# Recurrent cross-attention into a Serf feed-forward: batch 1's states loaded and turned apart, first products over six banks, a new written order

## The chip, the cores and the metric

One core of a Trainium2 chip. The core has a matrix engine (TensorE, "PE" in the profile), a vector engine (VectorE, "DVE"), a scalar engine (ScalarE, "ACT"), GpSimd ("POOL") and SyncE ("SP"). SP, POOL and, for two loads, ScalarE also issue DMA transfers. Engines run their own instruction lists in order and meet only at semaphores. The metric is the device time of one execution in microseconds (us), the median of several runs.

## The reference

Two stages. Attention reads x (8 batches, 8 heads, 512 tokens, 64 wide) against 32 states per head, both ways, and the two results are stacked to 544 rows per batch. A feed-forward layer with h·erf(softplus(h)) follows, 512 to 2048 to 512.

```python
def _attn_ref(x, state):
    scores = scale * np.matmul(x, state.transpose(0, 1, 3, 2))
    a = softmax(scores)                      # with 1e-9 in the sum
    xread = np.matmul(a, state)
    scores2 = scale * np.matmul(state, x.transpose(0, 1, 3, 2))
    a2 = softmax(scores2)
    sread = np.matmul(a2, x)
    return np.concatenate([xread, sread], axis=2)

def _moe_ref(x, w_in, w_out):
    h = x @ w_in
    sp = np.maximum(h, 0.0) + np.log1p(np.exp(-np.abs(h)))
    g = h * erf(sp)
    return g @ w_out
```

(The two softmax lines stand for the reference's maximum, exponential and sum.) Between the stages x becomes (4352, 512): per batch 512 token rows and 32 state rows.

## The kernel before

**Everything is a named step.** Functions register steps (a name and a closure). A hand-kept string, ORDER, lists their names, and the program issues them in that sequence. `in_order` then ties each instruction to the one ahead of it on its engine. So ORDER fixes the list of every engine and DMA queue; across engines only data dependences hold. An entry `~k*n` issues n filler products of the identity into bank k; they compute nothing that is used. `warm` is eight more at the start.

**How the work is laid out.** PSUM has eight banks of 128 x 512. Weights arrive as 64-bit words and are converted in pieces: `i0` to `i3`, `o0` to `o3` for the first half of the hidden width, with loads `l0`, `l1` (SP, `load_raw`, line 385), two ScalarE passes `a0`, `a1` (lines 370, 372) and two VectorE passes `v0`, `v1` (374, 376); two pieces share a buffer of raw words, so `o0l1` waits until `i0` is converted. Batches run one after the other: first all eight with one half of the hidden width (steps `A1` to `A7`; batch 0 in its own way), then the states' rows (`SA`, `SB`), then all eight with the other half (`B0` to `B7`).

**Batch 0**, `attention0` and `first_unit`. `lx0` to `lx3` and `lst0` load it. `x0` to `x3` turn x on TensorE; `s0` (line 448) puts the states on both halves of the partitions; `q0`, `q1` are the scores, copied by `q00c` and so on; `tm`, `max`, `less`, `exp`, `sum`, `inv`, `norm`, `ta`, `tac` are one softmax and its turning. `big`, `wt`, `wz`, `wn`, `tw0`, `tw1` (line 461) and ScalarE's copies `tw0c`, `tw1c` are the other softmax, and `rd0` (line 524) reads x with it; `rn0`, `rt0`, `rc0` keep the result. `n00` to `n12` (line 945) multiply states by w_in; `h0` to `h7` (line 956) are the first products of the feed-forward, each into one bank, from which ScalarE takes softplus (`h0s`, line 676) and a copy (`h0c`); `h0e` is the erf of h0 and h1, `h0g` their product on VectorE. `o00` to `o36` (line 977) are second products: first digit the row block, second the piece of the weights.

**Batches 1 to 7**, `attention(b)`. `a1xq0` to `a1xq7` load x once more by heads (line 349, two SP transfers of 64 KB each), `a1tx` turns them on VectorE, `a1s` (line 549) is the scores from the turned states `st[:, 1]` into banks 6 and 7, `a1c0`, `a1c1` (559) copy them. A chain on VectorE and ScalarE makes both softmaxes, up to `a1ta0`, `a1ta1`. `a1x0` to `a1x3` load x plain, into the place that batch 0's x had. `A1m` (line 638) multiplies states and w_in into banks 6, 7, 1 and 2, `A1m00` to `A1m11` copy it out on ScalarE, `A1f01` and on (line 687) are seven-product blocks of the hidden layer, `A1ap`, `A1bp` (810) of the output.

**The states of batches 1 to 7.** `hold`, a one-element copy on POOL, reads what `norm1` wrote. Behind it on POOL `lst1` to `lst8` (`load_st`, line 360) load the states, one transfer per head for all seven batches. `u1` and `u0` (line 1041) turn them on TensorE, seven transposes into banks 5 and 4, `u1c` and `u0c` copy them back over `st` on VectorE. POOL's other transfers (line 718) add results in DRAM; they begin after 100 us.

**Line numbers of helpers:** 246 copies, 238 to 240 sums, differences and products, 423 fillers, 418 and 419 `inverse`.

Of the kernel before, what the change touches and what calls it, by code (L numbers as in the profile page):

```python
# [31 lines left out]
a1ta1 a1ey1 o00 y11 A1M2 A1f0c y12 a1ty0 A1f06 a1ty1 h4e A1f02 y13 a1kz A1M3 A1f0u2 a1x3 A1f05 y14  # L32
o2a1 a2xq6 h4g A1f07 o2a0 a2xq5 o02 t32 A1M4 A1f0u3 o2v0 A1f0c11 A1f0c22 A1f04 h6e o3v0 a1z0 A1f11
o3a1 a1z3 o2v1 a1z1 A1f03 a1z2 A1f0c21 yl1 a2tx0 o04 A1f1c o3v1 A1f16 A1f0c12 A1f0s12 A1f12 T2
A1f0s22 A1f1u2 rd1 A1f0s21 t11 a1iy A1f0s11 t04 A1f17 h6g a2x3 rn10 rn11 A1f1c11 rt1 A1f15 A1f1u3
t34 rc1 T4 A1f14 o24 A1f1c22 A1e0 t61 a2tx2 A1f13 t21 t41 a2s A1f1c12 A1f1s22 t22 o06 A1g0 A1f1s11
a3xq1 a2c1 t1k A1f1c21 o14 a2c0 A1f1s12 a2tu0 o0c A1f1s21 o16 o0d t12 a2mx0 a2x2 a3xq7 A1e1 a2my0
o30 t3k yk0 a2sb0 a3xq5 o26 a3xq2 A1g1 a2ex0 a3xq0 A2m a3xq4 a2sm0 a2x0 o32 A2m00 t62 a3xq3 a2iz
A2m10 t42 a2nm0 A2m11 t2k o2c o34 a3xq6 a2ey0 A2M1 A2m01 a2ta0 a2x1 a2ey1 o36 A2M2 y21 A1q A2f01
o3c A2f05 A2f0c a2ty0 o1c y22 A1ap50 A1A1 A2f06 y23 A1ap10 a2ty1 A2f0u2 A2M3 A2f02 a2kz a2iy y24  # L40
A2f07 t24 T3 A1ap11 A2f0u3 A2f0c11 A1A3 A1ap51 A1ac A2f04 A2f0c22 A2M4 A2f11 A2f0c21 a2z3 t33 t4k
A2f03 t03 A2f1c a2z2 t51 a2z0 a3tx2 A1ap20 a2z1 yk1 A2f16 A2f0c12 o2d A2f0s12 o3d A1A2 A2f12
A2f1u2 o1d A2f0s22 yl2 A2f15 t13 yk2 A2f1c11 t23 A2f17 t6k a3tx0 rd2 A2f1u3 A1A4 A2f14 rn21 a3x2
rn20 t52 A1b2 rt2 A1ap21 rc2 A2f1c22 a3s A1ac11 A1a2 A2f13 a3c0 a4xq3 t43 t64 A2f1c21 A1ap60 A1a3
a3c1 a4xq2 A1ap61 A2f1c12 a3x0 A1bp10 t5k a3tu0 A1au2 a4xq0 A2f1s12 A1bp11 A2f0s21 t14 A1ap70 a3x1
a3mx0 A2f1s21 a3x3 A1ap71 A2f1s11 a4xq6 A1a4 A2f1s22 A3m A2f0s11 a4xq7 t44 A1au3 a3sb0 a4xq5
A1ap40 A1ac22 a3ex0 A1ap41 a3my0 A1ap30 A1ac21 t63 a3sm0 A1bc A1ap31 A3m01 A3m11 A1bp60 A1b3 a3ey1
A1bp61 a3iz A1ac12 A3m10 A1bp20 a3ey0 a3nm0 A1d2 A1bp50 A1bu2 a4xq4 A3m00 t53 A1bp51 a3ta0 A1bp21
A1bp70 t54 A2e0 y31 A1bp71 A3M1 A3f01 a3ty1 A3f05 a3ty0 A1bu3 A3f0c A3M2 A1bp40 a3kz A2e1 y32
A3f02 y33 A3M3 A3f06 A1bc22 A3f0c11 A1b4+ A1bp41 A1b4 A3f0u2 A3f11 A1bc21 y34 A1bc11 a3iy A2g0  # L50
A3f07 A1bp30 a3z1 A3f0u3 a3z3 a3z0 A1bp31 a3z2 A3f04 A3f0c22 A1d0 A3M4 a4xq1 A2ap10 A3f0c21 A1bc12
A1d3 A3f1c A3f03 A2g1 A1d1 A3f16 A3f12 A3f0s11 A3f0c12 A3f1u2 A1D0 rd3 A2q A3f0s21 A3f17 rn31 A1U2
rn30 rt3 A1D1 A2A1 A2ap50 A3f1u3 A3f0s12 A3f15 a4tx2 rc3 A2ap11 a4tx0 A3f14 A2ac A1U3 A2ap51 A2a2
A1D2 a4s A2A3 A2ap60 a4c1 a5xq1 a4c0 A3f1c22 A2ap61 a5xq0 A1D4 A2a3 A3f1c21 A3f13 A2au2 A1D3 a4x0
A3f1s12 a4tu0 A2ap20 A3f1c11 a5xq6 A2ap70 A3f1s22 A2A2 A2ap71 a4mx0 a5xq7 A2ap21 A2au3 A2A4 A2ap40
A2ac11 A3f1s11 A2ap41 a4sb0 A2bp10 A3f1c12 a4ex0 A2bp11 A2a4 A4m A2ac21 a4sm0 A2bc yl3 A2ac22
A2bp20 yk3 a4x2 a4iz A3f0s22 A2b2 A2bp21 a5xq4 A3f1s21 A2ap30 a4nm0 A4m01 A2bp60 A4m10 A4m11 A2b3
A2bp61 A4m00 A2ap31 a4ta0 A2bu2 a4x3 A2bp70 a4my0 A2bp71 A4f01 A2ac12 a4ey1 A4M1 A2d0 A2bp50 A2bu3
y41 a4ey0 a4x1 A4M2 A2bp51 A2d2 A4f0c A2bp40 y42 a5xq5 a4ty1 A2bp41 A4M4 A4f06 A3e0 a4ty0 A4f02
y44 a4kz A2b4 A2D0 yl4 A4f05 A4M3 A4f0c11 y43 A4f0u2 A2bc22 A4f11 A3e1 A2b4+ A3g0 A4f07 A2bp30  # L60
A4f0u3 A2bp31 A2bc11 a4z0 A4f04 A4f0c22 a4z2 a5xq2 A3g1 A4f03 A4f0c21 a4z1 A3ap10 A4f1c a4z3
A2bc21 a5xq3 A4f16 A4f0c12 A2d3 A4f12 a4iy A2bc12 A4f0s22 A3q A4f15 A2d1 A4f1u2 A4f17 A2U2 A3A1
rd4 A4f1u3 a5tx0 A4f14 rn40 rn41 A4f0s21 rt4 A3ap11 a5tx2 rc4 A3ap50 A3ac A4f1c22 A4f1c11 A3ap51
A3A3 A2D1 A4f1c21 a5s A3a2 A3ap20 a5c1 a6xq1 A2U3 A4f0s11 A3ap60 A3a3 A2D2 a5c0 A4f1s11 A3ap61
A2D3 A3A2 a6xq3 A4f13 a5tu0 A3ap21 a6xq2 A3au2 A2D4 A3ap70 A4f1c12 A3ac11 A3A4 A3ap71 a5x3 A3bp10
a5mx0 a6xq0 A3au3 A4f1s12 A3bp11 A3ac22 A4f1s22 A3ap40 A4f1s21 a5sb0 A3ap41 A4f0s12 A3a4 A5m a5my0
a5ex0 A3ap30 A3ac21 A3b2 A5m00 A3ap31 A3bc a5sm0 a5ey0 A3bp60 a5ey1 A3ac12 A3bp61 a5iz A5m11 A3d0
A3b3 A3bp50 A3bu2 a6xq4 A5m10 a5nm0 A3bp51 A3bp70 a6xq7 A3b4 A3bp71 a5x2 A4e0 a5ta0 A3bp20 a6xq6
A3bp21 A5M1 A3D0 A5f01 a5x0 A3bu3 y51 A5m01 A5M2 A3bp40 A5f0c a5ty0 A4e1 A3bp41 A3b4+ A5f02 y52
a5iy a5ty1 A5f06 A3bc11 A3bc22 a5kz A3bc21 A5f05 A5M3 a5x1 A5f0c11 y54 a6xq5 A5f0u2 A3bp30 y53  # L70
A4g0 A5f07 A3bp31 A5f0u3 A5f11 A5M4 A5f04 A5f0c22 a5z1 A4ap10 a5z3 A4g1 A5f0c21 a5z2 a5z0 A5f03
A5f1c yl5 yk5 A5f16 A3bc12 A5f12 A4q A5f1u2 A3d1 A3d2 A5f17 A5f1c11 A5f0c12 rd5 A4A1 A5f0s22 A5f15
a6tx0 rn51 rn50 A5f1u3 A4ap11 a6tx2 rt5 A3D1 A5f14 A4ac rc5 A5f1c22 A4ap20 A3d3 A3U2 a6x2 A4ap21
# [1077 lines left out]
```

## Time and profile before

| | |
|---|---|
| median of 3 runs | 689.32 us (688.62 to 690.2) |
| the profiled execution's own time | 691.2 us |
| its span, first to last instruction | 689.1 us |
| mean granted TensorE clock | 0.994 |
| DMA | 87.15 MB, mean 126 GB/s |
| instructions | 13808 |

A line of the busy table gives an engine's busy time, its share of the span and its instructions. The timeline gives start, duration, engine, line and operation, output and inputs, a count, and in brackets the idle time ahead of it with what ended it; durations include the pipeline's drain, so successive starts tell the pace. A stage row gives the stage, its length, busy time of TensorE, of its weight loads, of VectorE, ScalarE and POOL with instruction counts, then the granted TensorE clock (1.00 is full), the share of time in which the 16 DMA engines were busy, and GB/s. The time that a transfer takes to land is counted from its issue.

### The profile page before, as it was taken

How to read it: one execution, taken by the hardware profiler on the slowest of the kernel's cores; microseconds unless marked ns; L12 is line 12 of the kernel's file. 1: busy time of each engine (PE TensorE's matmuls, PEld its weight loads, DVE VectorE, ACT ScalarE, POOL GpSimd, SP SyncE). 2: the span in 40 equal slices, each digit the busy share in tenths (PEclk: the TensorE clock that was granted, in tenths of full speed). 3: DMA queues.
4: the chain of work that ended last, by engine and by line, in shares of the span. 5: the costliest groups of instructions: out<-in, count | busy, mean ns of one | idle time of the engine just before them, and what ended most of it. 6: DMA issues, size and time to landing. Idle time of an engine off the chain costs nothing.

```text
span 689.1 us, 13808 instructions
## 1 busy us (share of the span) xinstructions
PE 678.0 (98%) x5569; PEld 588.7 (85%) x5569; DVE 590.7 (86%) x771; ACT 489.5 (71%) x763; POOL 89.0 (13%) x84
## 2 busy tenths in 40 slices
...
GB/s 297 208 166 181 95 160 232 144 113 194 171 119 245 158 176 134 146 258 139 177 237 170 89 86 71 68 65 53 46 70 44 72 17 100 18 68 16 78 54 123
DMA packets 145567, 87.15 MB, mean 126 GB/s; under 512 B 92512, under 2 KB 137824, under 8 KB 145504
## 3 DMA queue, kind: packets, MB, share of 16 engines
...
q10 hardware_dynamic: 544, 0.52, 0.2%
q14 instruction: 19, 0.16, 0.1%
...
## 4 chain that ended last, share of the span: by engine, by line
PE 94%; DVE 2%; DMA 2%; ACT 1%; POOL 1%; issue 0%; DVEq 0%
PE b L810 47%; PE b L687 27%; PE b L740 5%; PE b L638 4%; PE b L1017 4%; PE b L977 3%; PE b L956 2%; DMA st<-in_state_dram 1%; PE b L524 1%; PE b L549 1%; POOL st L360 1%; DMA big<-in_x_dram 1%; PE b L1041 0%; PE b L461 0%; DVE ring L239 0%; DVE z L574 0%
## 5 line engine op out<-in xcount | busy, mean ns | idle before, releaser
L718 POOL DMA_DIRECT2D out_dram<-res x67 | 80.1, 1330 | 572.6 <-DVE res L238 179.7
L810 PE MATMUL b<-big,ring 128*128 128x128 f32 x1196 | 151.4, 275 | 0.0
L810 PEld LDWEIGHTS b<-big,ring 128*128 128x128 f32 x1196 | 144.9, 192 | 4.0 <-ACT res L246 1.0
L246 ACT COPY ring<-b 128x512 f32<-128x512 f32 (+1 forms) x144 | 82.7, 584 | 89.4 <-PE b L687 64.8
L687 PE MATMUL b<-y,m 128*128 128x256 f32 x480 | 121.3, 381 | 0.2 <-DVE y L246 0.2
L246 ACT COPY res<-b 128x512 f32<-128x512 f32 (+2 forms) x125 | 64.4, 524 | 53.9 <-PE b L810 37.3
L687 PEld LDWEIGHTS b<-y,m 128*128 128x128 f32 x480 | 86.5, 190 | 12.9 <-ACT ring L246 1.5
L687 PE MATMUL b<-sy,m 128*128 128x256 f32 x360 | 91.9, 380 | 0.0
L240 DVE TENSOR_TENSOR ring<-ring 128x2048 f32<-128x2048 f32 (+1 forms) x36 | 77.8, 2166 | 9.3 <-ACT ring L695 8.2
L676 ACT ACTIVATE ring<-ring 128x512 f32<-128x512 f32 x128 | 77.0, 632 | 1.0 <-DVE ring L238 0.5
L687 PEld LDWEIGHTS b<-sy,m 128*128 128x128 f32 x360 | 65.0, 190 | 9.0 <-issue 1.1
L810 PEld LDWEIGHTS b<-ta,ring 128*128 128x128 f32 x548 | 67.8, 192 | 5.5 <-issue 3.4
L810 PEld LDWEIGHTS b<-big,ta 128*128 128x128 f32 x572 | 68.9, 192 | 3.4 <-ACT res L246 1.7
L810 PE MATMUL b<-big,ta 128*128 128x128 f32 x572 | 71.8, 275 | 0.0
L810 PE MATMUL b<-ta,ring 128*128 128x128 f32 x548 | 71.8, 276 | 0.0
L239 DVE TENSOR_TENSOR ring<-ring 128x1024 f32<-128x1024 f32 (+3 forms) x66 | 68.8, 1046 | 0.1
L238 DVE TENSOR_TENSOR ring<-ring,b 128x512 f32<-128x512 f32 (+1 forms) x72 | 47.1, 658 | 25.3 <-PE b L687 8.7
L695 ACT ACTIVATE ring<-ring 128x2048 f32<-128x2048 f32 x30 | 57.4, 1913 | 0.2
L238 DVE TENSOR_TENSOR res<-res,b 128x512 f32<-128x512 f32 (+2 forms) x60 | 35.9, 599 | 24.2 <-PE b L810 14.3
L246 ACT COPY b<-b 128x512 f32<-128x512 f32 (+2 forms) x63 | 34.4, 548 | 16.6 <-PE b L810 12.3
L238 DVE TENSOR_TENSOR res<-res 128x512 f32<-128x512 f32 (+1 forms) x56 | 42.0, 751 | 0.8
L238 DVE TENSOR_TENSOR ring<-ring 128x1024 f32<-128x1024 f32 (+1 forms) x35 | 39.8, 1141 | 0.2
...
## 6 DMA issues: line engine op xcount, KB each, us to landing
...
big<-in_x_dram SPq DMA_DIRECT2D x112, 64.0 KB, 3.1
big<-in_moe_w_in_dram SPq DMA_DIRECT2D x12, 512.0 KB, 5.4
big<-in_moe_w_out_dram SPq DMA_DIRECT2D x12, 512.0 KB, 5.5
kept_y<-y SPq DMA_DIRECT2D x8, 512.0 KB, 4.1
y<-kept_y SPq DMA_DIRECT2D x8, 512.0 KB, 4.7
```

The costliest lines, as they stand in the source:

```text
L238: add = lambda o, a, b: tt(o, a, b, op=ALU.add)
L239: sub = lambda o, a, b: tt(o, a, b, op=ALU.subtract)
L240: mul = lambda o, a, b: tt(o, a, b, op=ALU.mult)
L246: do[name] = lambda: f(*args)
L638: pe.matmul(out=to[j][k][Ns * p:Ns * p + Ns, :], lhsT=by, rhs=w_in[r, 4 * j:4 * j + 4, i, :], start=True, stop=True)
L676: act.activation(out=o, in_=i, func=ACTF.Softplus)
L687: pe.matmul(out=to[:, i], lhsT=xs[n - 1][:, q:q + P], rhs=ys[n - 1], start=(start and i == 0), stop=(i == 1), skip_group_check=True)
L695: step(u + "e%d" % o, lambda s=s: act.activation(out=s, in_=s, func=ACTF.Erf))
L718: nc.gpsimd.dma_start(out=to, in_=of, accum_op=ALU.add)
L740: pe.matmul(out=to[:, E2 * h:E2 * h + E2], lhsT=a[:, k // 2, k % 2], rhs=rhs[n][:, k], start=(start and h == 0 and k == 0), stop=(k == 3), ...
L810: pe.matmul(out=out_[:, P * j:P * j + P], lhsT=lhs[:, i], rhs=rhs[:, i], start=(start and j == 0 and i == 0), stop=(i == 1), skip_group_ch ...
L1017: pe.matmul(out=to[:, P * i:P * i + P], lhsT=xs[n - 1][:, i, k], rhs=ys[n - 1][:, k], start=(start and i == 0 and k == 0), stop=(k == 1), ...
```

## The change

1. Batch 1's states get a load of their own on SP, `ls1` (64 KB), into the unused slot `st[:, 0]`. `ub` places them, in the form that `st[:, 1]` had, into bank 2 with four products against a rearranged identity; `ubc` copies them to `st[:, 1]` on VectorE.
2. `load_st` brings batches 2 to 7 only. `hold` now reads `sc` of batch 1, which `a1c0` writes, and stands behind `h5c`. `u0`, `u1` turn three batches each into banks 6 and 7, between `A1f02` and `A1f05`.
3. `h0` to `h7` use banks 0 to 5 in turn in place of 0 to 2.
4. The whole ORDER string is new, 2,511 entries after 2,516. It has the same steps but for `ls1`, `ub`, `ubc`, and 32 fillers after 33. The first lines of either are shown.

```diff
 ORDER = """
-warm lx0 lx1 lst0 lx2 lx3 i0l0 i1l1 i1l0 i0l1 x0 x1 x0c i2l0 s0 x1c x2 s0c i2l1 q0 x2c x3 q00c
-i3l1 q01c i0a0 big0 tm0 x3c i0v0 i0a1 q1 i3l0 max0 q10c i0v1 q11c less0 a1xq6 ~7*5 tm1 i1a1 big1
-n00 max1 exp0 i0+a0 less1 sum0 exp1 a1xq2 n00c0 sum1 i0+a1 i1a0 inv0 inv1 norm1 i2a0 norm0 hold
-~6*19 ta1 i1v0 lst1 i2a1 ta0 n00c1 lst6 i0+v0 i1v1 lst3 ta1c lst2 ta0c i0+v1 lst7 i3a0 o1l0 ~0*6
-n02 i2v0 lst4 n01 big n02c0 lst8 i2v1 i3a1 ~2*3 h0 lst5 n01c1 o0l1 n01c0 i3v0 wt0 o0l0 n02c1 n10
-wt1 a1xq3 i3v1 h1 n10c0 o1l1 n10c1 a1xq0 y01 wz n12 h0s wn1 h0c u1 n12c1 h1s u0 u1c n12c0 h1c wn0
-a1xq4 tw1 y02 u0c tw0 h0e a1xq1 h2 tw1c h0g a1xq5 tw0c o0a0 rd0 a1xq7 o1a0 o0v0 o3l0 h4 rn0 y04
-o1v0 yl0 a1tx1 rt0 o3l1 h3 h2s a1tx0 h2c a1tx2 o1a1 a1tx3 h5 o0a1 o1v1 rc0 h4c o0v1 a1s h4s h3c h7
-T1 h3s a2xq4 a1c0 a1c1 t01 o2l0 a1tu0 h5c a2xq3 h6 h5s a1my0 h7c t0k a1mx0 h7s a2xq1 a1tu1 o10 h6s
-a1my1 a2xq0 a1mx1 a2xq2 A1m a1sb0 h2e t31 a1x0 a1sb1 a2xq7 h2g o20 a1ex0 a1x2 t02 a1ex1 a1sm0 a1x1
-A1m10 o22 o2l1 a1sm1 A1m01 A1m11 a1iz y03 a1ey0 a1nm0 o12 a1nm1 A1m00 h6c a1ta0 o3a0 A1M1 A1f01
...
+warm lx0 lst0 lx1 lx2 lx3 i0l0 i0l1 i1l1 i1l0 x0 s0 x1 s0c x0c x2 x1c i2l0 q0 x2c x3 q01c i2l1
+q00c i0a0 big0 tm0 x3c i0v0 ls1 i0a1 max0 q1 i0v1 q11c q10c less0 i3l0 ~7*5 tm1 big1 exp0 n00
+i0+a0 max1 i3l1 i0+a1 sum0 i1a0 less1 inv0 a1xq6 big exp1 norm0 n00c0 sum1 i1a1 ~6*13 ta0 inv1
+n00c1 norm1 a1xq4 ta0c i1v0 wt0 ~7*4 ta1 i0+v0 i2a0 i1v1 ub ta1c i0+v1 ~6*4 n02 a1xq1 i2a1 i2v0
+n01 o0l1 y01 n02c0 i2v1 wt1 o0l0 ~5*4 h0 a1xq0 n01c0 i3a0 n01c1 n02c1 a1xq5 n10 i3a1 i3v0 o1l0 h1
+n10c1 n10c0 i3v1 wz ~7*2 n12 h1s wn1 a1xq7 h1c h5 wn0 n12c0 h0s y02 o1l1 ubc a1xq3 n12c1 tw0 a1tx0
+h0e tw1 a1tx2 a1xq2 h0c h3 y04 tw1c o3l0 h0g tw0c o0a0 rd0 a1tx3 o0a1 o0v0 h4 a1x1 rn0 a1x3 o1a0
+o0v1 o3l1 o2l0 rt0 o1a1 h2 o1v0 a1tx1 rc0 a1x2 t01 a1s o1v1 yl0 h4s h6 h2s T1 a1c0 h5c hold a1tu0
+h5s h7 lst8 t31 a1c1 a1mx0 o2l1 lst5 h3s a2xq5 a1tu1 h2c o20 h3c t02 a2xq2 a1my1 h7c h6s t04 t0k
+a1mx1 h7s o00 a1sb0 a1sb1 h2e t32 A1m t3k y03 a2xq0 t34 h2g lst1 a1x0 lst2 a1ex1 a1my0 a2xq4 o02
+a1ex0 lst3 a1sm1 a1ey0 a2xq1 a1sm0 a1ey1 o22 a1iz a1nm0 h4c A1m00 a1nm1 a2xq3 h6c o10 a1ta0 A1m11
+a1ta1 lst7 A1m10 y11 o3a0 lst6 a1ty0 A1f01 lst4 a1ty1 A1m01 o12 A1M1 A1f0c a1kz o2a0 y12 a2xq6
+A1M2 A1M3 o2a1 A1f06 a1iy y13 A1f02 o2v0 A1f0u2 y14 u0 o2v1 A1f07 h4e A1M4 u1 t61 A1f0u3 A1f05 h4g
+A1f0c11 a1z2 A1f04 o3a1 a1z3 A1f0c22 a1z0 A1f11 a1z1 o3v0 A1f0c21 yl1 t11 h6e o24 a2xq7 o3v1 A1f1c
+u0c A1f16 a2tx0 A1f03 A1f0s11 u1c A1f1u2 A1f12 T2 A1f0s12 A1f17 A1f0s22 A1f0c12 A1f1c11 rd1 A1f1u3
+T4 A1f1s11 A1f15 rn10 t12 a2x2 rn11 A1f0s21 t21 t1k rt1 h6g A1f14 a2x0 yk0 o04 A1f1c22 A1e0 a2tx2
+A1f13 t62 rc1 t22 a2s A1g0 A1f1s22 o06 a3xq0 a2c1 a2c0 A1f1c12 a2x1 A1f1c21 yk1 o14 a2tu0 o0c
+A1f1s12 a3xq4 A1f1s21 t41 a2mx0 o26 a3xq5 a2my0 A1e1 o16 a2sb0 a2x3 t4k A1g1 o30 a3xq2 a2ex0 A2m
+a2ey0 a3xq3 a2sm0 a2ey1 a3xq6 t14 o32 a2iz A2m10 a2iy t2k a2nm0 A2m11 o2c A2M1 o1c o34 o2d A2m00
...
 
     def load_st(h):
         i, e = h // 2, h % 2
-        nc.gpsimd.dma_start(out=st[Ns * i:Ns * i + Ns, 1:B, D * e:D * e + D],
-                            in_=state[1:B, h].rearrange("b n d -> n b d"))
+        nc.gpsimd.dma_start(out=st[Ns * i:Ns * i + Ns, 2:B, D * e:D * e + D],
+                            in_=state[2:B, h].rearrange("b n d -> n b d"))
+
+    def load_st1():
+        nc.sync.dma_start(out=st[:, 0].rearrange("p (g d) -> p g d", g=2),
+                          in_=state[1].rearrange("(g h) n d -> (h n) g d", g=2))
 
 
 
...
             step("norm%d" % g, lambda g=g: mul(a[g], a[g], over(Z1[:, g])))
             step("ta%d" % g, four, tp[g], lambda c, g=g: A0[:, g, c].rearrange("p q n -> p (q n)"))
             step("ta%dc" % g, act.copy, y[0][:, g], tp[g])
-        step("hold", lambda: nc.gpsimd.tensor_copy(out=sn[:, 0, 0:1], in_=A0[:, 1, 0, 0, 0:1]))
-        for h in range(H):
-            step("lst%d" % (h + 1), load_st, h)
 
         def rest():
             for e in range(2):
...
         for e in range(2):
             step(name("c%d" % e), lambda e=e: act.activation(
                 out=sc[:, e], in_=bank[6 + e], func=ACTF.Copy, scale=scale))
+        if b == 1:
+            step("hold", lambda: nc.gpsimd.tensor_copy(out=sn[:, 0, 0:1], in_=sc[:, 0, 0:1]))
         parts = [(str(e), slice(e, e + n)) for e in range(0, 2, n)]
         a = lambda e: both[:, e].rearrange("p e (k n) -> p (e k) n", n=Ns)
         M = lambda e: M1[:, e].rearrange("p e k -> p (e k)")
...
                 mixed_part(g, f, n, to)
             for i in range(4):
                 k = 4 * g + i
-                to = bank[k % 3]
+                to = bank[k % 6]
                 step("h%d" % k, first, g, i, to)
                 step("h%ds" % k, soft, s[:, k], to)
                 step("h%dc" % k, act.copy, hs[:, k], to)
...
     for j in range(4):
         piece("i", j)
     rest0 = attention0()
-    for k, bs in enumerate((range(1, 5), range(5, B))):
-        def turn_states(bs=bs, k=k):
-            for n, b in enumerate(bs):
-                pe.transpose(out=o_bank[2 + k][:, P * n:P * n + P], in_=st[:, b, :],
-                             identity=ident)
-        step("u%d" % k, turn_states)
-        step("u%dc" % k, dve.tensor_copy, st[:, bs[0]:bs[-1] + 1].rearrange("p b t -> p (b t)"),
-             o_bank[2 + k][:, 0:P * len(bs)])
+    step("ls1", load_st1)
+
+    def turn_st1():
+        by = ident.rearrange("p (a e n) -> p e a n", a=2, e=2)
+        for g in range(2):
+            for e in range(2):
+                pe.matmul(out=bank[2][D * e:D * e + D, D * g:D * g + D],
+                          lhsT=st[:, 0, D * g:D * g + D], rhs=by[:, e], start=True, stop=True)
+    step("ub", turn_st1)
+    step("ubc", dve.tensor_copy, st[:, 1], bank[2][:, 0:P])
     seconds0 = first_unit()
     for j in range(4):
         piece("o", j)
...
     attention(1)
     sums_y(1)
     mixed("A1", 1)
+    for h in range(H):
+        step("lst%d" % (h + 1), load_st, h)
+    for k, bs in enumerate((range(2, 5), range(5, B))):
+        def turn_states(bs=bs, k=k):
+            for n, b in enumerate(bs):
+                pe.transpose(out=bank[6 + k][:, P * n:P * n + P], in_=st[:, b, :],
+                             identity=ident)
+        step("u%d" % k, turn_states)
+        step("u%dc" % k, dve.tensor_copy, st[:, bs[0]:bs[-1] + 1].rearrange("p b t -> p (b t)"),
+             bank[6 + k][:, 0:P * len(bs)])
     hidden("A1", 1, 1)
     sums_a("A1", 1, twice=TWICE < 2)
     seconds0()
```

More of the change, by code (lines that the diff above doesn't have):

```diff
@@ L32 @@
[L32 to L73, printed above, removed]
@@ new lines @@
+a3ex0 a4xq7 A1b2 A1ap30 a3sm0 A1ap31 A2f0s22 A3m A1b3 A1ac21 a3iz A1bc t63 A2f1s21 a3nm0 A1bp60
+A3m00 A1ac12 A3m10 A1bp61 A3m11 a3ta0 A1bp20 A1d3 A2f0s21 A1d0 A1bp21 A1bu2 a3x1 t53 A3m01 A3f01
+a3iy a3x0 a3ty0 A2f1s12 A1bp70 A3M1 A3f0c a3ty1 A2f1s22 A1bp71 t64 A1bp50 a3kz A1bu3 y31 A3M2
+A1bp51 a4xq4 y33 A3f02 y32 A2e1 t54 A3f06 A3M3 A1D0 t44 A3f05 A1bc22 A3f0u2 A1b4 A1bp40 A2e0 y34
+A1b4+ A3f07 A2g1 A1bp30 A3f0u3 a3z2 A1bp31 A3f0c11 a3z1 A3f04 a3z3 A3f0c22 a3z0 A3f11 yk2 A3M4
+A3f0c21 A1d2 A1bc12 A1bp41 A3f1c A2g0 A3f03 A1bc11 A1bc21 A3f16 A1d1 A3f12 A3f1u2 A3f0c12 A2ap10
@@ new lines @@
+A5f05 y53 A5f0u2 A3b4+ A3bc21 A3bp30 A5M4 yl5 A4g0 A5f07 A5f11 a5z1 A5f0u3 a5z2 A3bp31 a5z3
+A5f0c22 a5x1 A5f04 A3D0 a5z0 A3bc12 yk5 A4ap10 A4g1 A5f0c21 A3d1 A5f1c A5f03 A5f16 A5f0c12 A5f12
+A5f1u2 A3U2 A5f15 A4q A5f17 A5f0s22 a6tx0 A4ap50 A5f1u3 A5f0s21 A4A1 rd5 a6tx2 A5f14 A3D1 rn51
+a6x1 rn50 rt5 A4ap11 A5f1c22 rc5 A4a2 a6s A4ac A4A2 A5f13 a6c0 a7xq4 a6c1 A4ap60 A4A3 A5f1c11
+A5f0s11 A4ap61 A3U3 A5f1c21 A4ap20 A4a3 A3D3 A4au2 A4ap21 A5f1s12 A3D2 a6tu0 a7xq1 A5f1s22 A4ap70
+A3D4 A4ac11 A4A4 A4ap71 A4bp10 a6mx0 A4au3 A5f1s11 A4bp11 A5f1c12 A4ap40 a6sb0 a6x3 A4ap41 a7xq0
@@ new lines @@
+A7f01 y71 A5d0 a7my0 a7x0 A5bp50 A5d2 A7f0c A5bp51 A6e0 y72 A7M2 A7f02 y73 A7f06 A7M4 yk7 A5bu3
+y74 A7f05 A7M3 A7f0u2 A5bc22 A5bp40 A5b4 A7f07 A6g1 a7ey1 A5D0 A5bp30 A5bc11 A7f0u3 A5bp31 A7f0c11
+A7f04 a7ey0 A5bc12 A7f0c22 A7f11 A6g0 A7f0c21 A5bp41 A7f1c A7f03 A5bc21 A7f16 A5d1 A6q A7f12
+A7f1u2 A6ap10 a7ty1 A7f0c12 A7f17 a7ty0 A7f15 A7f1u3 A6A1 a7kz i5+a1 A6ap50 A7f1c22 A7f14 A5U2
+A5D1 A6ap11 A6a2 A7f13 A6ac A5U3 A6ap51 A6A2 A6ap60 A7f1s22 A6A4 A7f0s12 A6ap61 A7f1c11 a7z3
+A6ap20 a7z1 A7f1c21 A6a3 a7z2 A6au2 a7z0 A5D4 A6ap21 yl7 A6A3 A6ap70 A5D2 A6ac11 A7f0s21 A6b2
```

218 lines of the change are left out of this document (117 added, 101 removed).

## The prediction

> **What bounds the kernel now.** I read the page first: busy times and the chain that ended last.
>
> ```profile
> span 689.1 us, 13808 instructions
> ...
> PE 678.0 (98%) x5569; PEld 588.7 (85%) x5569; DVE 590.7 (86%) x771; ACT 489.5 (71%) x763; POOL 89.0 (13%) x84
> ...
> PE 94%; DVE 2%; DMA 2%; ACT 1%; POOL 1%; issue 0%; DVEq 0%
> ```
>
> TensorE is the bound: it is busy 98% of the span and 94% of the chain. The number of its real instructions hardly changes, so the time can fall only by its idle time, by slow clock, or by filler products. The waits of TensorE, longest first, say where it is idle:
>
> ```profile
> PE b L1041 <- DMA st<-in_state_dram: 4.1, 1, 4.1
> ...
> PE b L687 <- DVE y L246: 0.2, 1, 0.2
> ```
>
> Columns: total, times, longest. One wait counts: line 1041 (steps u1, u0, the turning of the states of batches 1 to 7) stands 4.1 us for the state loads. Around it the timeline, the chain's pieces and the stage table show:
>
> ```profile
> 16.84 0.58 POOL L486 COPY sn<-ring 128x1 f32<-128x1 f32 x1 [15.53 <-DVE ring L240]
> 17.36 5.78 POOL L360 DMA_DIRECT2D st<-in_state_dram  x8
> 26.22 0.66 PE L945 MATMUL b<-w_in,st 64*32 64x256 f32 x16
> 30.98 1.73 PE L1041 MATMUL b<-ident,st 128*128 128x128 f32 x7 [4.09 <-DMA st<-in_state_dram]
> 32.49 1.91 PE L461 MATMUL b<-ident,ring 128*128 128x128 f32 x8
> ```
>
> ```profile
> 22.18 8.66 DMA st<-in_state_dram
> ```
>
> ```profile
> 27.00:31.00 4.00, 0.02 (x1) 0.06 (x1) 0.42 (x1) 3.77 (x6) 0.00 (x0) 0.81 0.89 186
> 31.00:37.00 6.00, 6.00 (x19) 4.21 (x19) 3.71 (x6) 3.14 (x4) 0.00 (x0) 0.56 0.65 102
> ```
>
> POOL begins the eight state loads at 17.36, behind the step hold. The last of them lands 8.66 us after the last issue. TensorE had finished line 945 (n12) at 26.22 + 0.66 = 26.88 and starts u1 at 30.98. Stage rows give TensorE, weight loads, VectorE, ScalarE, POOL, then the granted clock. In 31 to 37 us the clock is 0.56 on average: TensorE is "busy" for 6.00 us but does 6.00 x 0.56 = 3.36 us of work at full speed. So the stall costs 4.10 us idle + 2.64 us slow clock = **6.74 us**. After that:
>
> ```profile
> 45.00:100.00 55.00, 54.84 (x306) 30.66 (x305) 52.97 (x83) 49.00 (x73) 0.00 (x0) 1.00 0.64 147
> 100.00:200.00 100.00, 100.00 (x968) 87.90 (x974) 98.19 (x128) 74.94 (x124) 12.20 (x10) 1.00 0.76 169
> 200.00:300.00 100.00, 100.00 (x932) 88.62 (x913) 97.61 (x124) 74.93 (x122) 13.30 (x11) 1.00 0.77 172
> ```
>
> TensorE never waits again at full clock, but VectorE is 96 to 98% busy too (52.97 of 55, 98.19 and 97.61 of 100). It is nearly a second bound up to 300 us.
>
> [...]
>
> **The change part by part, against the profiled execution's own 691.2 us (span 689.1, 2.1 outside it).** The median of the three runs, 689.32, is 1.9 lower; a saving is taken off both alike.
>
> (a) *Batch 1's states apart.* ls1 is one more load of 64 KB on SP, ahead of i3's loads and all a1xq loads. The bounds are its twin lst0 and the slowest load of that time (columns: KB each, us to landing):
>
> ```profile
> ring<-in_state_dram SPq DMA_DIRECT2D x1, 64.0 KB, 3.8
> ring<-in_moe_w_in_dram SPq DMA_DIRECT2D x4, 512.0 KB, 9.4
> 1.25 0.45 SPq L341 DMA_DIRECT2D ring<-in_state_dram  x1
> 5.29 6.39 SPq L385 DMA_DIRECT2D ring<-in_moe_w_in_dram  x4
> 6.25 0.66 PE L448 MATMUL b<-ident,ring 128*64 128x128 f32 x8
> ```
>
> It holds SP for 0.45 us. It stands behind two of the four loads that took 6.39 us from 5.29, so it is issued by 5.29 + 3.2 = 8.5 and lands between 12.3 (8.5 + 3.8) and 17.9 (8.5 + 9.4). ub stands behind n00, 13 fillers, ta0, 4 fillers and ta1. The ta-steps need norm, whose end released hold at 16.84 before, and take 0.95: ub is due near 18. Its wait is nothing by either bound, though by the slower one without cover; a microsecond more is rival C. ub itself is four products like line 448's four (0.66 us) but half as wide: 0.3 to 0.66, taken 0.45. One transpose less in u0 and u1 gives 0.12 back, since line 461's eight take 1.91 at half clock, 0.95 at full. ubc is one more VectorE copy of 128 columns (about 0.3 us), between wn0 and n12c1, hidden unless VectorE is late there.
>
> (b) *Fillers.* 33 before (5, 19, 6, 3), 32 after (5, 13, 4, 4, 4, 2). Five take 1.38 us with the drain, so one is about 0.24 us:
>
> ```profile
> 10.47 1.38 PE L423 MATMUL b<-ident 128*128 128x128 f32 x10
> ```
>
> (a) and (b) on TensorE: +0.45 - 0.12 - 0.24 = **+0.1 us**. n12 would end near 27.0.
>
> (c) *u1 and u0 leave the early path.* After n12 TensorE now runs h5, tw0, tw1, h3, rd0, h4, rt0, h2, a1s. The first thing to come late is rd0, which needs ScalarE's copies tw1c and tw0c:
>
> ```profile
> 26.10 0.60 ACT L676 ACTIVATE ring<-b 128x512 f32<-128x512 f32 x1
> 28.45 1.28 ACT L971 ACT_TABLE_LOAD   x1
> 29.74 1.06 ACT L971 ACTIVATE ring<-ring 128x1024 f32<-128x1024 f32 x1
> 33.59 0.59 ACT L246 COPY ring<-b 128x512 f32<-128x512 f32 x1 [2.80 <-PE b L461]
> 34.20 2.91 PE L956 MATMUL b<-y,m 128*128 128x512 f32 x4
> 37.05 1.10 PE L524 MATMUL b<-big,ring 128*32 128x64 f32 x64
> 40.01 3.60 PE L956 MATMUL b<-y,m 128*128 128x512 f32 x8
> 43.53 1.09 PE L549 MATMUL b<-big,st 64*32 64x512 f32 x16
> ```
>
> ScalarE worked without a gap from h0s (26.10) to the end of h0e (29.74 + 1.06 = 30.80), then idled 2.80 us. The same steps stand ahead of tw1c in the new order (h0c now behind h0e), so the two copies end near 30.8 + 2 x 0.59 = 32.0. TensorE: two h-steps take 3.5 us (40.01 to 43.53), one 1.75; 27.0 + 1.75 (h5) + 0.95 (tw0, tw1) + 1.75 (h3) = 31.45. So rd0 waits 0.5 us (nothing to 1.2). Then 32.0 + 1.05 (rd0) + 1.75 (h4) + 0.1 + 1.75 (h2) gives a1s at 36.6, against 43.53. Of these 6.9 us, 0.8 are u1 and u0, which now come later: **6.1 us** gained here. a1s also needs the turned a1xq loads. SP issues ten of them in 10.76 us and they land 3.1 us later:
>
> ```profile
> 11.81 6.30 SPq L349 DMA_DIRECT2D big<-in_x_dram  x4
> 24.46 10.76 SPq L349 DMA_DIRECT2D big<-in_x_dram  x10
> big<-in_x_dram SPq DMA_DIRECT2D x112, 64.0 KB, 3.1
> ```
>
> In the new order six go out behind i3l1 (four before, at 1.6 us each), so until about 21; then o0l1 and ten more, among three weight loads of 0.45. That ends between 33 and 34, lands near 36.5, and a1tx1 (0.6) follows: a1s at 36.6 to 37.3. I take 36.7, **6.0 us**.
>
> (d) *From a1s to A1f01*, which waited for VectorE in the run of before (57.36). ScalarE fills this stretch:
>
> ```profile
> 35.00:56.30 21.30, 21.30 (x152) 8.87 (x151) 17.77 (x30) 19.69 (x32) 0.00 (x0) 0.97 0.74 170
> 48.09 1.88 PE L977 MATMUL b<-ta,ring 128*128 128x512 f32 x4
> 49.90 1.95 PE L638 MATMUL b<-w_in,st 64*32 64x512 f32 x32
> 57.36 1.10 PE L687 MATMUL b<-y,m 128*128 128x256 f32 x4 [0.16 <-DVE y L246]
> ```
>
> ScalarE needs 19.69 of the 21.30 us between tw0c and A1f01's inputs. From 32.0 that is 51.7 without any gap and 53.3 with the gaps of before. TensorE has a1s (1.0, from 43.53 to the next h-step), seven h- and o-steps of 1.75 (line 977's, 48.09 to 49.90, is one) and A1m (line 638, 1.9): 36.7 + 1.0 + 12.2 + 1.9 = 51.8. I take 52.3. Ahead of A1f01 the new order has one o-step more (1.72) and the u-steps (0.8) not yet: gain 57.36 - 52.3 + 0.9 = 5.96 (5.0 to 6.6).
>
> (e) *The other states on POOL*, hold now behind a1c0 (ScalarE's copy of the scores). POOL has nothing else until past 100 us (0.00 busy in 45 to 100), so nothing queues behind hold but the loads themselves. a1c0 ends near 38.9; from hold's start to the landing it took 30.98 - 16.84 = 14.1 us, so the states are there at 53.0. u0 comes after A1f01, o12, A1f06 and A1f02. An A1f-step is four products of line 687, which the chain's pieces give in sixteens:
>
> ```profile
> 60.17 3.45 PE b L687 x16
> ```
>
> So 3.45 / 4 = 0.86 each, and u0 is due at 52.3 + 0.86 + 1.72 + 1.72 = 56.6. Cover 3.6 us; if it is gone, rival B's price holds. u0 and u1 write banks 6 and 7, emptied by A1m00 and A1m01 shortly before.
>
> (f) *Six banks for h0 to h7*: on three banks the h-steps met one wait, of the weight load alone:
>
> ```profile
> PEld b L956 <- ACT ring L676: 0.8, 1, 0.8
> ```
>
> TensorE's own list does not have it; taken as nothing, a gain of 0.8 to a loss of 0.2 (the wait for y).
>
> (g) *The new order from 60 us to the end* changes the sequence, not the set, of steps. The row of before is "no wait"; bounds nothing to 2 us, taken 0.1.
>
> Sum: 6.0 - 0.1 = **5.9 us**; profiled execution 685.3, median 689.3 - 5.9 = **683.4**. Own range: gain 4.6 to 7.0, 682.3 to 684.7.
>
> **The rivals.**
>
> *A. VectorE caps the gain.* For it: 45 to 300 us leaves it about 6 us idle in all, and its regained time is bounded: idle 3.58 us in 27 to 31 and 2.29 in 31 to 37, together 5.9, exactly what TensorE gains. Wherever the new order puts VectorE work a little earlier than TensorE's need, TensorE waits. Against: TensorE had only one 0.2 us wait for it. If half the regained time is lost again: gain 3, **686.3**.
>
> *B. The stall moves to u0, and the kernel is slower.* Place: u0, behind the landing of the eight POOL loads. [...] The decisive point is a landing later than 56.6, and for a loss one later than 56.6 + 3.3 = 59.9: 3.3 us idle plus 2.6 us slow clock eat the gain. That is 21 us after hold, against 14.1. At 5 us idle: 689.3 - 5.9 + 5 + 2.6 = **691.0**. Against: the transfers of that time load the DMA engines to 0.74 (the share in the row for 35 to 56.3), those of before stood beside 1.04:
>
> ```profile
> 17.00:27.00 10.00, 9.49 (x99) 4.97 (x97) 8.94 (x18) 9.40 (x16) 6.13 (x9) 1.00 1.04 260
> ```
>
> [...]
>
> *C. The split does not free ub.* ls1 is queued behind six loads of 512 KB; if it lands after 18 us, ub waits and everything behind it: 1.5 us, gain 4.4, **684.9**. Against: it is as small as its twin, and only the slower bound comes near.
>
> **How the numbers follow.** Forecast 0.60, A 0.17, B 0.13 (of it 0.04 near no change, 0.09 slower), C 0.06, and 0.04 that the reordered rest has waits that cost over 5 us (0.01 same, 0.03 slower). About 0.2% (1.4 us) is what this kernel's runs can tell from no change. Faster = 0.60 + 0.17 + 0.06 = 0.83, cut to 0.82 for the tail of A; same 0.06 (B and the rest give 0.05, A's tail the other 0.01); slower 0.12. The range leaves out the slower part of B and the last case and reaches from 681.8 (gain 7.5: no wait at rd0, h-steps better) to 688.3 (A at its worst).
>
> **What would show it.** u1's wait gone from TensorE's list; granted clock 1.00 in 27 to 45; a1s near 36.7, A1f01 near 52.3, u0 near 56.6 without a wait; last state landing near 53; TensorE's tail unchanged. Wrong if TensorE's list shows a new wait over 1 us, at u0 (B), at line 549 or 687 for VectorE (A), or at ub (C), or if a second stretch of clock 0.50 appears.

## The result and the profile after

| | median | runs |
|---|---|---|
| before | 689.53 us | 12 |
| changed kernel | 686.75 us | 12 |
| ratio | 0.996, 95% interval 0.9946 to 0.9974 | |
| again, in another session: before 689.32, changed | 686.13 us | 26 and 9 |
| its ratio | 0.9957, interval 0.9944 to 0.9971 | |

The change makes the kernel about 3 us faster (2.8 and 3.2), where 5.9 was forecast. One of its first twelve executions, the profiled one, took 3722 us for a reason that stays open; what follows reads another profiled execution of the same kernel, of 686.48 us.

The page of that execution, in the places that were shown of before (span, busy times, the chain by engine):

```profile
span 684.4 us, 13822 instructions
...
PE 676.4 (99%) x5574; PEld 587.9 (86%) x5574; DVE 592.0 (86%) x772; ACT 493.5 (72%) x766; POOL 87.8 (13%) x84
...
PE 93%; ACT 3%; DVE 3%; issue 1%; DVEq 0%; ACTq 0%
```

The 4.1 us wait for the states is gone. ScalarE and VectorE now hold 3% of the chain each. The waits of TensorE (total, times, longest):

```profile
PE b L427 <- PEq L1150: 0.8, 1, 0.8
PE b L980 <- DVE ring L240: 0.5, 1, 0.5
PE b L465 <- DVE ring L246: 0.4, 1, 0.4
PE b L690 <- ACT ring L246: 0.3, 1, 0.3
PE b L465 <- DVE ring L240: 0.3, 1, 0.3
PE b L525 <- ACT ring L246: 0.3, 1, 0.3
PE b L690 <- DVE m L239: 0.3, 1, 0.3
PE b L460 <- DVE big L246: 0.2, 1, 0.2
```

Before had one wait of 4.1 us and three of 0.2 to 0.5 us (the 0.8 us of the start, PEq, stands in both); now there are seven of 0.2 to 0.5 us. (Lines moved by one to four: 980 was 977, 690 was 687, 465 was 461, 525 was 524.) The timeline of TensorE and of POOL at the points that the prediction named:

```profile
12.67 0.45 PE L948 MATMUL b<-w_in,st 64*32 64x128 f32 x16
18.44 0.45 PE L1047 MATMUL b<-ident,st 128*64 128x64 f32 x8
27.26 1.98 PE L959 MATMUL b<-y,m 128*128 128x512 f32 x4
32.11 1.10 PE L525 MATMUL b<-big,ring 128*32 128x64 f32 x64 [0.27 <-ACT ring L246]
36.88 1.31 PE L550 MATMUL b<-big,st 64*32 64x512 f32 x16
47.58 5.42 PE L980 MATMUL b<-ta,ring 128*128 128x512 f32 x12 [0.45 <-DVE ring L240]
52.84 1.03 PE L690 MATMUL b<-y,m 128*128 128x256 f32 x4
55.84 1.10 PE L690 MATMUL b<-sy,m 128*128 128x256 f32 x4 [0.26 <-DVE m L239]
57.64 0.49 PE L1064 MATMUL b<-ident,st 128*128 128x128 f32 x3
60.52 1.13 PE L690 MATMUL b<-sy,m 128*128 128x256 f32 x4 [0.32 <-ACT ring L246]
```

```profile
39.55 0.18 POOL L563 COPY sn<-big 128x1 f32<-128x1 f32 x1 [38.24 <-ACT big L560]
39.67 4.71 POOL L360 DMA_DIRECT2D st<-in_state_dram  x8
```

From above: n00, ub, h5, rd0, a1s, o02 to o10, A1f01, A1f06, u0, A1f04. ub and u0 start without a wait. The stage table (stage, length, TensorE, weight loads, VectorE, ScalarE, POOL, clock, DMA share, GB/s):

```profile
27.00:31.00 4.00, 4.00 (x31) 2.26 (x16) 2.74 (x7) 3.97 (x7) 0.00 (x0) 1.00 0.79 187
31.00:37.00 6.00, 5.73 (x79) 2.57 (x83) 5.50 (x9) 5.98 (x9) 0.00 (x0) 1.00 1.00 261
26.00:52.00 26.00, 25.28 (x185) 11.18 (x184) 23.27 (x44) 25.64 (x42) 4.83 (x9) 1.00 0.95 235
45.00:62.00 17.00, 15.96 (x82) 9.06 (x82) 16.11 (x31) 16.57 (x26) 0.00 (x0) 1.00 0.82 174
```

The clock stays at 1.00 where it was 0.56. In 26 to 52 us ScalarE is busy 25.64 of 26 us: its list has almost no gap left. In 45 to 62 TensorE is idle 17 - 15.96 = 1.04 us, all of it in the three marked waits; before it stood 0.16 there. The chain of work that ended last says who set the pace. It leaves TensorE behind an h-step, runs on ScalarE from 26.33 to 48.22 us, then on VectorE up to A1f06, and comes back to TensorE there. Three of its pieces (start, length, engine, output and line):

```profile
26.33 0.60 ACT ring L679
48.24 1.29 DVE z L577 x2
55.84 1.12 PE b L690 x4
```

### The profile page after: what moved, and what is told of

It is laid out like the page before. It is cut to its first block, busy times and chain, and to the rows that moved or that the text cites. A ratio compares the mean times of both kernels' runs of the same rounds, so it can differ in the third digit from the quotient of the medians.

```text
span 3720.2 us, 13822 instructions
## 1 busy us (share of the span) xinstructions
PE 3714.4 (100%) x5574; PEld 2927.6 (79%) x5574; DVE 601.4 (16%) x772; ACT 502.8 (14%) x766; POOL 87.8 (2%) x84
## 4 chain that ended last, share of the span: by engine, by line
PE 100%; DVE 0%; DVEq 0%; issue 0%
PE b L813 46%; PE b L690 28%; PE b L743 5%; PE b L980 5%; PE b L641 4%; PE b L1020 4%; PE b L959 2%; PE b L427 1%; PE b L525 1%; PE b L550 1%; PE b L465 0%; PE b L948 0%; PE b L445 0%; PE b L535 0%; PE b L460 0%; PE b L1064 0%
## 5 line engine op out<-in xcount | busy, mean ns | idle before, releaser
L813 PEld LDWEIGHTS b<-big,ring 128*128 128x128 f32 x1196 | 742.4, 846 | 59.0 <-issue 57.5
L813 PE MATMUL b<-big,ring 128*128 128x128 f32 x1196 | 746.1, 951 | 0.0
L690 PE MATMUL b<-y,m 128*128 128x256 f32 x480 | 638.4, 1622 | 0.0
L690 PEld LDWEIGHTS b<-y,m 128*128 128x128 f32 x480 | 400.5, 869 | 156.3 <-issue 156.3
L690 PE MATMUL b<-sy,m 128*128 128x256 f32 x360 | 476.1, 1618 | 0.0
L813 PEld LDWEIGHTS b<-ta,ring 128*128 128x128 f32 x548 | 368.5, 907 | 28.3 <-issue 27.4
L690 PEld LDWEIGHTS b<-sy,m 128*128 128x128 f32 x360 | 295.9, 854 | 117.1 <-issue 116.7
L813 PE MATMUL b<-ta,ring 128*128 128x128 f32 x548 | 371.2, 1011 | 0.0
L813 PEld LDWEIGHTS b<-big,ta 128*128 128x128 f32 x572 | 324.6, 781 | 24.3 <-issue 24.3
L813 PE MATMUL b<-big,ta 128*128 128x128 f32 x572 | 325.5, 880 | 0.0
L980 PEld LDWEIGHTS b<-ta,ring 128*128 128x128 f32 x64 | 55.0, 879 | 109.4 <-issue 107.5
L743 PEld LDWEIGHTS b<-big,ring 128*128 128x128 f32 x104 | 72.6, 704 | 43.7 <-issue 43.7
```

Of the source, the lines that this page charges most:

```text
L690: pe.matmul(out=to[:, i], lhsT=xs[n - 1][:, q:q + P], rhs=ys[n - 1], start=(start and i == 0), stop=(i == 1), skip_group_check=True)
L743: pe.matmul(out=to[:, E2 * h:E2 * h + E2], lhsT=a[:, k // 2, k % 2], rhs=rhs[n][:, k], start=(start and h == 0 and k == 0), stop=(k == 3), ...
L813: pe.matmul(out=out_[:, P * j:P * j + P], lhsT=lhs[:, i], rhs=rhs[:, i], start=(start and j == 0 and i == 0), stop=(i == 1), skip_group_ch ...
L980: pe.matmul(out=bank[3 + r % 3], lhsT=s[:, k, P * r:P * r + P], rhs=wo[0].w[:, k, :], start=(k == 0), stop=(k == NT - 1))
```

## The experiments

**1. How much does before lose at u1?** Before, unchanged, was profiled five times more, beside the kernels below; e_banks has its order too.

> The kernel of before again, to see how much the stall at u1 varies. Theory 1: a wait of 2 to 4 us at u1 and, when it is under about 2.5 us, no stretch of half clock, so a loss between 2 and 6.7 us. Theories 2 and 3: the same 4 us and half clock as in the first profile, since they put the missing gain into the new kernel.

> Before, unchanged, another profile. Theory 1 (the stall at u1 is different in every execution, and its price sets the time): the wait at u1 lies between 1.5 and 4.5 us; span less (wait + slow-clock loss) is 682 to 683 us, as in the profiles so far (689.1 - 6.7; 687.1 - 4.7). Theory 2 (the stall is the same and something later varies): the wait is 4 us whatever the span.

> Before, unchanged, one more profile. The same as for the last: Theory 1: span less (wait at u1 + slow-clock loss) 682 to 683 us. Theory 2: a wait of 4 us whatever the span.

> Before, unchanged, another profile. Theory 1 (early loads land differently in each execution, and what they cost sets the time): waits of TensorE for states or for weights between 17 and 37 us, with slow clock, of 3 to 7 us in all, and span less these 682 to 683.5 us. Theory 2 (the first profile is typical): u1 waits 4 us and the span is 689 us.

> Before, unchanged, one more profile. As for the last: Theory 1: 3 to 7 us of waits and slow clock between 17 and 37 us, span less these 682 to 683.5 us. Theory 2: u1 waits 4 us and the span is 689 us.

The waits of b_again, and then those of b_p2:

```profile
PE b L1041 <- DMA st<-in_state_dram: 1.6, 1, 1.6
PE b L956 <- ACT m L246: 1.3, 1, 1.3
...
PE b L461 <- DVE ring L501: 0.3, 1, 0.3
```

```profile
PE b L956 <- ACT m L246: 1.6, 1, 1.6
PE b L524 <- ACT ring L246: 1.0, 1, 1.0
```

b_p2 has no wait at u1 at all. It waits at h0 for n02c0, because ScalarE stood for a load of w_in ahead of it (i3), and then loses to slow clock. ScalarE's timeline and the stage row show it:

```profile
22.45 1.12 ACT L370 ACTIVATE w_in<-ring 128x1024 f32<-128x1024 f32 x1 [1.57 <-DMA ring<-in_moe_w_in_dram]
```

```profile
24.00:27.50 3.50, 3.50 (x5) 0.96 (x6) 1.85 (x3) 2.44 (x6) 0.00 (x0) 0.51 1.00 316
```

All seven profiles of before's order, with the waits of TensorE between 17 and 37 us and what the clock took ((1 - clock) x length of its stage rows):

| | span | u1 | h0 | rd0, tw | slow clock | span less these |
|---|---|---|---|---|---|---|
| first profile | 689.1 | 4.1 | - | - | 2.6 | 682.4 |
| e_banks | 687.1 | 3.0 | - | - | 1.7 | 682.4 |
| b_again | 685.4 | 1.6 | 1.3 | 0.3 | - | 682.2 |
| b_p2 | 688.3 | - | 1.6 | 1.3 | 1.7 | 683.7 |
| b_p3 | 687.3 | 2.2 | 0.9 | - | 1.7 | 682.5 |
| b_p4 | 685.8 | 1.8 | 0.8 | 0.3 | - | 682.9 |
| b_p5 | 685.3 | 0.6 | 1.2 | 0.7 | - | 682.8 |

The right column lies within 1.5 us (0.7 without b_p2) while the spans lie 3.8 us apart; the span follows what is lost early. (Five of the seven also wait 0.3 us at line 945, which is left in the column.) So Theory 2 falls, and b_again's Theory 3 with it: the first profile was the dearest of seven, not a typical one.

Theory 1 holds in kind, but only in the wider form that b_p4 and b_p5 state, with every early wait counted. In its first form, the stall at u1 alone, it missed: b_again waits 1.6 us there where 2 to 4 were asked, b_p2 not at all, and the span less u1's wait and slow clock is 686.6 us in b_p2 and 683.4 in b_p3, where 682 to 683 were asked. b_p4 and b_p5 keep the stated 682 to 683.5, but lose 2.9 and 2.5 us where at least 3 were asked; b_p2's remainder, 683.7, lies just outside even so.

A median run of before has a span of about 689.4 - 2.1 = 687.3, so it loses 687.3 - 682.7 (mean of the right column) = **4.6 us**, not 6.74; the seven profiles lose 4.2 on average. What makes the loads land so differently was not tried.

**2. The changed kernel again.**

> The changed kernel again, for a profile with TensorE at its usual pace. Theory 1 (the mechanism holds, the price is smaller): 686 to 687 us, no wait of TensorE over 1 us, granted clock 0.998 or more, a1s between 36.5 and 39 us; what is missing of the 5.9 us lies in waits of 0.3 to 1 us at rd0, a1s and A1f01, and in a run of before that had lost more than usual. Theory 2 (VectorE or ScalarE caps the gain): TensorE waits 2 us or more in all for VectorE or ScalarE between 27 and 300 us. Theory 3 (the stall moved): one wait of 2 us or more at u0 or ub for a load.

686.13 us, and the profile above: no wait over 0.5 us, a1s at 36.88. Theory 3 falls, as ub and u0 do not wait. Theory 2 asks for 2 us or more of waits for VectorE or ScalarE after 27 us; there are 0.27 + 0.45 + 0.26 + 0.32 = 1.30 us, so its cause is there and its price is not reached. Theory 1 has the time, the clock and a1s right, and of its places rd0; the other waits stand at o02, A1f06 and A1f04, not at a1s and A1f01.

Counted like the seven, and with the late waits, this profile leaves 684.4 - 0.55 (0.28 at ta1, 0.27 at rd0) - 1.03 (the three waits after 45 us) = 682.8 us, within 0.1 of before's mean remainder. So what the changed kernel still waits accounts for what it did not gain, in this one profile.

**3. Its parts alone.** e_banks is before with one edit. e_split is before's order with the split; only the moved steps are shown:

```diff
-                to = bank[k % 3]
+                to = bank[k % 6]
```

```diff
- ... i2l1 i3l1 ... norm0 hold ~6*19 ta1 i1v0 lst1 ... ta0 n00c1 ... ~2*3 h0
+ ... i2l1 ls1 i3l1 ... norm0 ~6*19 ta1 i1v0 ... ta0 ub n00c1 ... ~4*3 h0
- ... y01 wz n12 ... u1 n12c1 h1s u0 u1c ... u0c ... a1c0 a1c1 t01 ... A1f02 y13
+ ... y01 ubc wz n12 ... n12c1 h1s ... a1c0 a1c1 hold lst8 ... lst4 t01 ... A1f02 u0 y13
```

> Before with six banks for h0 to h7 and nothing else. All theories: within 0.5 us of before, as no wait of TensorE for an h-step's bank stood in the profile; the stall at u1 stays. If it gains 1 us or more, banks belong to the gain.

> Before's order and three banks, with the split of the states alone: ls1 behind i2l1, ub behind ta0, ubc behind y01, hold and the eight loads behind a1c1, u0 and u1 behind A1f02 and A1f07. Theory 1: the stall at u1 is gone by this part alone, rd0 waits 1.5 us instead; 2.5 to 4.5 us faster than before. Theory 2: 1 to 3 us faster, with new waits for VectorE after 45 us. Theory 3: no faster, with a wait at ub or u0.

> Before's order and three banks with the split of the states alone, as in e_states, and the three fillers ahead of h0 in bank 4, so that they leave ub's result in bank 2 alone. Theory 1: as e_states, 687.3 to 688 us, with about 1.4 us of wait at rd0 for tw0c; the rest of the change's gain comes from the new order. Theory 2 (the order adds nothing): within 0.3 us of the changed kernel.

e_banks: 689.38 against 689.32 us, ratio 1.0005 (0.9993 to 1.0017): nothing, as all theories had it. e_states: 687.59, ratio 0.9976 (0.9966 to 0.9986), 1.7 us faster. Its Theory 1 had rd0's wait right (1.4 us in its list) but asked for 2.5 to 4.5 us, a miss; Theory 2's 1 to 3 us is met, without the new waits for VectorE after 45 us that were to cause it. In e_states the three fillers write into bank 2 between ub and ubc, so batch 1's states are the identity there; e_split puts them into bank 4 and has 687.41 us, 0.9977 (0.9965 to 0.9988). So the split alone gains 1.7 us (689.13 - 687.41 in its own session). The waits of e_split:

```profile
PE b L522 <- ACT ring L243: 1.4, 1, 1.4
...
PE b L956 <- ACT m L243: 0.8, 1, 0.8
PE b L462 <- DVE m L243: 0.6, 1, 0.6
```

With the stall gone, rd0 (line 522 there) waits 1.4 us for ScalarE's copies tw1c and tw0c, and h0 still waits 0.8 us for a ScalarE copy (n02c0). Theory 1's two numbers hold. The rest goes with the new order: 686.13 and 686.75 against 687.41, though the intervals of the ratios just overlap (0.9944 to 0.9974 against 0.9965 to 0.9988). The traces show where: it runs h5 and h3 ahead of rd0, which waits 0.27 us, and it puts ScalarE's passes over i3 behind n02c0, on which h0 waits: no h0 wait stands in its list. Six banks without this order gain nothing, but the order needs them: on three banks h2 would have to write bank 2 while h5's sum, which h5c reads later, still stands there. The new order on three banks was therefore not tried.

**4. The waits that are left.** Five orders of the changed kernel; three have one edit each:

```diff
 a_sums:   - a1ty0 A1f01 lst4 a1ty1 A1m01 o12 A1M1 A1f0c a1kz o2a0 y12 a2xq6 A1M2
           + A1M1 A1M2 y12 a1ty0 A1f01 lst4 a1ty1 A1m01 o12 A1f0c a1kz o2a0 a2xq6
 a_h4e:    - h4e A1M4 u1 t61 A1f0u3 A1f05 h4g A1f0c11
           + A1M4 u1 t61 A1f0u3 A1f05 A1f0c11 h4e h4g
 a_start:  - x0 s0 x1 s0c x0c x2 x1c
           + x0 x1 s0 x0c x1c s0c x2
```

a_tuned is a_sums and a_h4e together, a_both is a_start and a_sums. a_start also puts lst0 behind lx1 and q00c ahead of q01c.

> The changed kernel with two moves in its order: A1M1, A1M2, y12 ahead of a1ty0, and h4e, h4g behind A1f0c11. Theory 1 (the waits at line 690 of 0.26 and 0.32 us, at A1f06 and A1f04, are part of what is missing): both go, 0.3 to 0.6 us faster than the changed kernel. Theory 2 (ScalarE's and VectorE's load only shifts): the waits return behind A1f04 at other lines, within 0.2 us of the changed kernel.

> The changed kernel with A1M1, A1M2, y12 ahead of a1ty0 alone, half of a_tuned. Theory 1: the wait of 0.26 us at line 690 goes and the time falls by 0.1 to 0.3 us. Theory 2: the wait returns behind, within 0.1 us; the loss of a_tuned is not here.

> The changed kernel with h4e, h4g behind A1f0c11 alone, the other half of a_tuned. Theory 1: the whole loss of a_tuned comes from here, 2 to 3 us slower than the changed kernel, with a wait of about 1.9 us at o24 for h4g. Theory 2 (the loss is spread over both moves): under 1.5 us slower.

> The changed kernel with before's order of the first loads, turns and copies (x0 x1 s0, x0c x1c s0c, q00c q01c). Theory 1 (the later start of n00, 12.67 against 12.21 us, is passed on to the end): 0.3 to 0.5 us faster than the changed kernel, no wait at q0 and tm0. Theory 2 (ScalarE's list sets a1s and swallows it): within 0.2 us of the changed kernel.

> a_start and a_sums together. Theory 1: 0.4 to 0.8 us faster than the changed kernel, near 685.5 us; faster than both kernels. Theory 2: within 0.3 us of the changed kernel.

| | median | ratio to before, interval |
|---|---|---|
| changed kernel | 686.13 | 0.9957 (0.9944 to 0.9971) |
| a_tuned | 689.10 | 1.0000 (0.9987 to 1.0013) |
| a_sums | 686.26 | 0.9955 (0.9940 to 0.9971) |
| a_h4e | 688.44 | 0.9995 (0.9979 to 1.0010) |
| a_start | 686.47 | 0.9963 (0.9950 to 0.9975) |
| a_both | 686.23 | 0.9957 (0.9943 to 0.9971) |

a_tuned lost the whole gain, and a_h4e says where: the two waits that it adds, TensorE's for h4g and for a ScalarE copy, and VectorE's own:

```profile
63.45 1.99 PE L977 MATMUL b<-ta,ring 128*128 128x512 f32 x4 [1.87 <-DVE ring L237]
66.19 1.13 PE L687 MATMUL b<-sy,m 128*128 128x256 f32 x4 [0.75 <-ACT b L243]
```

```profile
62.17 1.23 DVE L237 TENSOR_TENSOR ring<-ring 128x1024 f32<-128x1024 f32 x1 [2.60 <-ACT ring L971]
```

The erf of h4 and h5, moved 2 us later on ScalarE to spare A1f04 a wait of 0.32 us, made VectorE stand 2.60 us for it and o24 wait 1.87 us for VectorE. Theory 1 of a_h4e holds, and both theories of a_tuned fall. a_sums removed its wait of 0.26 us, and its list has 0.18 us more at line 687 for a ScalarE copy. a_start has n00 at 12.34 us against 12.67, but that start is no sure effect of the order: before's own profiles have it between 11.78 and 12.52. Neither of the two, nor both together, shows a gain; the 0.1 to 0.8 us that their Theories 1 ask for are less than intervals of about 1 us to either side can tell. None of these orders beats the changed kernel.

**5. Does ScalarE hold TensorE there?** In a_noerf the step h2e issues nothing, so its output differs in the columns of h2 and h3.

```diff
-                step("h%de" % k, lambda k=k: act.activation(
+                step("h%de" % k, lambda k=k: None if k == 2 else act.activation(
```

> The changed kernel without the erf of h2 and h3 (step h2e issues nothing, so its product uses softplus itself). ScalarE is spared 1.06 us and the 1.28 us table load ahead of it, between a1s and A1f01. Theory 1 (ScalarE's list holds TensorE between 45 and 62 us): the waits at line 980 for h2g (0.45) and at line 690 (0.26 and 0.32) shrink or go, A1f01 starts 0.4 us or more earlier, 0.5 to 1.1 us faster than the changed kernel. Theory 2 (VectorE holds it): the waits at line 690 stay, under 0.3 us faster.

685.63 us, ratio to before 0.9943 (0.9924 to 0.9961). TensorE's list has lost the waits for h2g (line 980) and for the sums (line 690, VectorE):

```profile
PE b L690 <- ACT ring L246: 0.3, 1, 0.3
PE b L465 <- DVE ring L240: 0.3, 1, 0.3
PE b L525 <- ACT ring L246: 0.3, 1, 0.3
```

In the changed kernel's profile h2g had stood for ScalarE's erf of h2 and h3 (line 974), and o02 for h2g:

```profile
46.30 1.22 DVE L240 TENSOR_TENSOR ring<-ring 128x1024 f32<-128x1024 f32 x1 [0.51 <-ACT ring L974]
```

Without that erf the chain of a_noerf stays on TensorE from 34.44 us to A1f06, where the changed kernel's ran on ScalarE and VectorE:

```profile
36.16 2.41 PE b L550 x16
47.51 5.35 PE b L980 x12
55.44 1.09 PE b L690 x4
```

From the h-step behind a1s to A1f04 TensorE takes 60.09 - 38.50 = 21.59 us, against 60.52 - 38.12 = 22.40 in the changed kernel. So ScalarE's list held TensorE in the first two of the three waits; the third, 0.32 us, stayed. Not all of Theory 1 came: A1f01 starts only 0.14 us earlier (52.70), although a_noerf had begun 0.8 us ahead. There a1s took 2.48 us in place of 1.31, because ScalarE had stood 1.10 us for a load of w_out and copied late. And the 0.5 us between the medians lie within the intervals of the two ratios, so how much time ScalarE's list costs is not settled.

## Why the prediction was half right

**What held.** The path was as worked out, to within 0.6 us up to A1f01 and 1.2 us at the end:

| | forecast | measured |
|---|---|---|
| end of n12 | 27.0 | 27.33 |
| rd0, and its wait | 32.0, 0.5 | 32.11, 0.27 |
| a1s | 36.7 | 36.88 |
| A1f01 | 52.3 | 52.84 |
| u0 | 56.6 | 57.64 |
| profiled span | 683.2 (689.1 - 5.9) | 684.4 |

(a) ub had no wait; rival C did not come. (c) The slow clock went with the stall (1.00 in 27 to 37 us), and rd0 was the next to come late, for tw0c. (d) ScalarE's list was the bound, up to 48 us and then through VectorE. (e) The eight loads were issued by 44.4 us (39.67 + 4.71) and u0, 13 us later, did not wait; rival B did not come. The eight issues took 4.71 us against 5.78 before, of 48 KB each against 56. (f) Six banks alone: nothing.

**What failed: "a saving is taken off both alike".** The 6.74 us were right for the profiled execution, and from its own span the change saved 689.1 - 684.4 = 4.7 us. But that execution was 1.9 us slower than the median because its stall was dearer. The saving cannot be subtracted from a median that never had it. With 4.6 us for a usual loss the same sum gives 4.6 - 0.8 = 3.8 us, 685.5. That is 2.1 of the 2.7 to 3.4 us by which the forecast of 683.4 was off (medians 686.13 and 686.75).

**The rest, 0.6 to 1.3 us, is a term sized too small.** Step (d) allowed TensorE to reach A1f01 half a microsecond late, and (g) gave 0.1 us to everything after 60 us. No term stood for the stretch between A1f01 and 60 us. Measured: 0.45 us at o02, which made A1f01 0.5 us later than the forecast took it, then 0.26 at A1f06 and 0.32 at A1f04. Together that is 1.1 of the 1.2 us between 5.9 and the 4.7 us that the change saved against the first profile. Rival A had the kind of loss right, with the wrong engine at its head (ScalarE, 98.6% busy from 26 to 52 us, then VectorE behind it) and more than twice the size (2.9 us). That its 686.3 lies beside the measured medians is luck: most of what it put down to VectorE was the dear draw of the first profile. After 62 us the two kernels differ by nothing that a wait shows.

**Two details.** u1 and u0 wrote banks 2 and 5 before, not 5 and 4 as the section on the kernel has it, and the new order has 2,516 entries after 2,511, not the other way round. No step hung on either.
